# Routed attention with a SoLU layer: the hand-written order of five queues and transfers, written anew up to the middle of the third batch

## The chip, the cores and the metric

The kernel runs on one core of a Trainium2 chip. Five engines of that core take part, each with a queue of its own that it works through strictly in order: TensorE (PE in the profile; its weight loads are listed apart as PEld), VectorE (DVE), ScalarE (ACT), GpSimd (POOL) and SyncE (SP), which does no arithmetic here and issues nearly all DMA transfers. The metric is the device time of one execution in microseconds (us). Three executions of the kernel before took 224.7, 224.66 and 224.9 us, a median of 224.7 us.

## The reference

Attention in which a query sees only the keys of its own cluster, and then a feed-forward layer with a softmax-weighted activation (SoLU) and a layer norm. Batch 4, 8 heads, 768 tokens, head size 64, 16 clusters; the layer is 512 to 1024 to 512 on 3072 tokens.

```python
q_assign = np.argmax(np.einsum('bhsd,hcd->bhsc', q_n, c_n), axis=-1)   # q_n, c_n: unit length
k_assign = np.argmax(np.einsum('bhsd,hcd->bhsc', k_n, c_n), axis=-1)
mask = q_assign[:, :, :, None] == k_assign[:, :, None, :]
scores = np.where(mask, scale * np.matmul(q, k.transpose(0, 1, 3, 2)), -1000000000.0)
attn = softmax(scores)                      # written out in full in the reference
x = np.matmul(attn, v)                      # then all heads of a token side by side
h = x @ w_in
solu = h * softmax(h)
ln = (solu - mean(solu)) / np.sqrt(var(solu) + 1e-06) * g_ln
out = ln @ w_out
```

## The kernel before

**The work.** The kernel goes through 16 pairs of heads, (batch 0, pair 0) to (batch 3, pair 3). For a pair, q and k are loaded and turned (by PE in batch 0, by a VectorE block transpose after that), the tokens are compared with the centroids, and the one-hot cluster of each token is put below the 64 rows of q and k, so that one matmul gives masked scores. The scores of all pairs form 288 banks of PSUM; for each bank, PE computes scores, ScalarE takes the exponential, and PE multiplies the exponentials with v. The v tile has a column of ones behind its 64 columns, which gives the row sums; VectorE divides by them. The feed-forward layer takes 128 tokens at a time, 24 groups: a transposing DMA of x, `h` on PE, its maximum on VectorE, an exponential on ScalarE, the product on VectorE, a second transposing DMA, `y` on PE with statistics taken beside it, a scaling on ScalarE or VectorE, and the store.

**The planner.** Nothing in the program is issued in the order of its text. Every piece of work is put with `add` into a list under a name: the kind, and behind it the batch, pair, bank or group. The class `Weave` then reads a text of kinds for every engine (`ORDER["PE"]` and so on). An entry such as `S3` in it takes the next three operations of that kind from those that belong to the engine, in the order in which they were added. So the texts alone set the order of each queue. The table `AWAY` moves single operations to another engine than the one given in `add`. The durations given in `add` (and the model in `run`) only set the order in which instructions of different engines are written out; on the chip, each queue runs on its own and waits for semaphores.

**The kinds that the prediction speaks of**, with the line that issues the work in the profile:

| kind | engine | work | line |
|---|---|---|---|
| `S`, `E`, `V` | PE, ACT, PE | scores of one bank (2 matmuls; in the first 24 banks one narrower matmul); its exponential; 6 matmuls with v | L613, L621, L638 |
| `N` | DVE | reciprocal and product: divides a group of `V` by the row sums | L650, L663 |
| `h`, `hm`, `ex`, `u` | PE, DVE, ACT, DVE | a quarter of the first product of a group (2 matmuls); maximum; exponential; product | L724, L730, L736, L743 |
| `tx`, `tu` | SP | the transposing DMAs of x and of u | L693, L748 |
| `y`, `sc` | PE, ACT or DVE | a quarter of the second product (2 matmuls); scaling | L788, L803, L805 |
| `al` | POOL | two small operations for the scaling | L770, L773 |
| `cl` | PE | comparison with the centroids (8 matmuls) | L453, L458 |
| `ot`, `pl`, `bl` | DVE; POOL, DVE, ACT or SP | one-hot turned; put in its place; a block cleared | L502, L524, L533 |
| `tp`, `xa` | PE, ACT or DVE | turning q and k of batch 0; taking them out of PSUM | L394, L401 |
| `ca`, `cv` | POOL, DVE, ACT | q or k of one head to bf16; v to bf16 | L439 to L443, L542 |
| `z` | POOL | the column of ones of a v tile | L1246 |
| `ld`, `lv` | SP | loads of q and k, of v | L407, L537 |

Three rings matter. A score bank is free again when its exponential is done, and there are three such banks, so `S` waits for the `E` three banks earlier. The first `V` of a group of units waits for the `N` of the group before. The products `y` share one PSUM bank (tag `m`) with `cl`, so each waits for the scaling or the transpose that empties it. There are six v tiles; `z1` to `z5` set the ones in the second to the sixth, each once in the whole kernel, and the first `V` that reads a tile waits for its `z`:

```python
def clear(z):
    nc.gpsimd.memset(v1[z][:, :, :, D:], 1.0)
```

`z5` belongs to the tile of pair (1,1), whose first `V` is the one named `V28.0`. In POOL's text it stands, as counted out to names, in this neighbourhood:

```text
ca1.1.1.1 ca1.2.0.0 ca1.2.0.1 al1 z5 at2 ca1.2.1.0 al2
```

Of the kernel before, what the change touches and what calls it, by code (L numbers as in the profile page):

```python
# [22 lines left out]
class Weave:  # L23
# [21 lines left out]
    ORDER["PE"] = """
        fl wm fl tp2 cp fl2 cl tp fl tp fl4 cl S3 tp2 S2 tp2 cq S2 tp S tp S2 tp S cl S2 V S
        tp S V S V S gt V S V2 S cl S V S V S V S tp S tp S2 tp S V S tp V2 S2 cl S3 V2 S V
        S V S2 V S V2 S2 V S cl S3 V2 S V S V S su S3 V2 S V S V S su S3 V2 S V2 S2 me S3 V2
        S V S V S cl S2 V S V S V2 S2 h S h S2 h2 S V2 S2 h V2 S h S V2 S2 h S V S V S h S h
        S2 V S h V S y2 V2 S2 y V S V S h3 S3 y V3 h V S2 V2 S cl S3 h2 S2 V3 S y2 S V h2 S  # L50
        V y2 S h S V h S2 h S y3 S2 y V3 h S3 cl V2 S V S y S2 y2 S3 V3 S y S2 V3 S2 cl S V
        S2 V2 S h S2 V2 S V S h S2 V2 cl V2 S3 y2 S V S2 V y S2 y V2 S3 h2 S V h S h S2 V h
        S V S V y2 S h V y2 S2 V S h3 S cl V S2 V2 S h V cl S3 h2 V y V S3 y2 V S h V3 S y S
        h S2 h2 S3 V2 y h S V S2 y V3 y S3 h3 y S3 V3 S h S V S V cl S V S h S cl V2 S3 y V2
        S y S2 y V2 S3 h y V S3 V h V2 S3 cl S2 V2 S y3 S2 y S V3 S V S y S2 V S V3 S2 y2 S3
        y V2 S2 h V2 S3 h3 S V S2 V y S V h2 V2 S y S2 y V y S h2 S3 cl h V S2 V3 S h V2 S3
        h2 S y S2 V h S2 V y2 V4 S3 y h S2 h V h V S V S y2 S3 V3 h2 S2 h2 S2 y2 S V S h2 S
        V3 S2 h S h S2 V S y V2 S V y2 S2 h2 S2 h2 V2 S2 V2 y S2 h V2 h V S2 h S V h S3 V2 h
        y S V y3 V h3 S2 y3 S2 y h2 V2 h y h y3 h V h V y4 h ptx h y4 h2 y3 h2 y ptu2 y6 ptu
        y ptu y5  # L60
    """
# [28 lines left out]
    AWAY.update(dict.fromkeys("""  # L90
        ca0.0.1.0.0 ca0.0.1.0.1 ca0.0.1.1.0 ca0.0.1.1.1 pl0.0.0.0.1 pl0.0.1.0.0 pl0.0.1.1.0
        pl1.0.0.0 pl1.0.0.1 pl1.0.1.0 pl1.0.1.1 pl1.1.0.0 pl1.1.0.1 pl1.1.1.0 pl1.1.1.1
        pl1.2.0.0 pl1.2.0.1 pl1.2.1.0 pl1.2.1.1 pl1.3.0.0 pl1.3.0.1 pl1.3.1.0 pl1.3.1.1
        pl2.0.0.0 pl2.0.0.1 pl2.0.1.0 pl2.0.1.1 pl2.1.0.0 pl2.1.0.1 pl2.1.1.0 pl2.1.1.1
        pl2.2.0.0 pl2.2.0.1 pl2.2.1.0 pl2.2.1.1 pl2.3.0.0 pl2.3.1.0 pl2.3.1.1 pl3.0.0.0
        pl3.0.0.1 pl3.0.1.0 pl3.0.1.1 pl3.1.0.1 pl3.1.1.0 pl3.1.1.1 pl3.2.0.0 pl3.2.0.1
        pl3.2.1.0 pl3.3.0.1 pl3.3.1.0 pl3.3.1.1
    """.split(), "POOL"))
# [1182 lines left out]
```

## Time and profile before

| what | value |
|---|---|
| median of three executions | 224.7 us (224.66 to 224.9) |
| the profiled execution, its own time | 224.64 us |
| its span, first to last instruction | 222.7 us |
| granted TensorE clock | 0.997 |
| PE busy, instructions | 216.4 us (97%), 2420 |
| DVE busy, instructions | 196.8 us (88%), 355 |
| ACT busy, instructions | 192.0 us (86%), 372 |
| POOL busy, instructions | 130.3 us (59%), 251 |
| HBM read and written | 23.11 MB, 6.29 MB |

In rows of the profile, L12 is line 12 of the kernel; `out<-in` names the tiles by the program's own names; `xN` counts instructions. A row of the timeline gives the start, the duration, engine, line and operation, and in square brackets how long the engine stood idle before it and what ended that. Matmuls are pipelined and their ends are modelled, so a full busy column of PE does not say that PE lost nothing; the distance from start to start does. Two instructions on ACT or DVE overlap a little, so the mean of one is longer than the step from one to the next. A row of the chain of waits gives the start, the time and the work on the chain that ended last.

### The profile page before, as it was taken

To read this page: it belongs to the slowest core of one execution; us is meant where nothing else is said; L and a number is where in the kernel's file an instruction comes from. 1 tells how busy PE (TensorE), PEld (TensorE's weight loads), DVE (VectorE), ACT (ScalarE), POOL (GpSimd) and SP (SyncE) were. 2 spreads that over 40 slices of the span, in tenths; PEclk is the share of its full clock that TensorE was granted. 3 is DMA by queue.
4 is the path that set the end of the run, shared out by engine and by line. 5 is a ranking of instruction groups with operands and counts; after the bars stand their busy time and mean duration, and the time that the engine had idled before them with its cause. 6 is when DMAs were issued, how large, how long until landed. Compare 5 with 4: busy or idle time off the path is not lost.

```text
span 222.7 us, 6609 instructions
## 1 busy us (share of the span) xinstructions
PE 216.4 (97%) x2420; PEld 147.9 (66%) x2420; DVE 196.8 (88%) x355; ACT 192.0 (86%) x372; POOL 130.3 (59%) x251
## 2 busy tenths in 40 slices
PE   7999999999999999999999999999999999999993
PEld 4667657666766678776677667777677677755452
DVE  4899997999999989999998989887999889888982
ACT  2699999999997999998889898999999998983362
POOL 3699881970887989547678534953895403032331
PEclk9999999999999999999999999999999999999998
DMA  6999989995898989899998999199930434486713
GB/s 148 353 268 261 278 173 316 243 214 99 126 249 140 232 141 175 189 199 174 178 244 146 174 201 191 66 213 202 236 59 16 92 62 129 92 144 161 183 70 133
DMA packets 125679, 38.80 MB, mean 174 GB/s; under 512 B 115016, under 2 KB 121168, under 8 KB 125648
## 3 DMA queue, kind: packets, MB, share of 16 engines
q1 hardware_dynamic: 123904, 37.87, 80.0%
q10 hardware_dynamic: 1744, 0.52, 1.0%
q8 instruction: 19, 0.31, 0.6%
q14 instruction: 12, 0.10, 0.1%
HBM read 23.11 MB, written 6.29 MB: 132 GB/s over the span
## 4 chain that ended last, share of the span: by engine, by line
PE 93%; ACT 1%; DVE 1%; issue 1%; POOL 1%; DVEq 0%; ACTq 0%
PE sps L613 30%; PE hreg L724 18%; PE yps L788 18%; PE ops L638 15%; PE csc L458 4%; PE hreg L394 2%; PE idle_p L832 2%; ACT e L621 1%; PE csc L453 1%; PE hreg L584 1%; PE hreg L788 1%; PE utp L712 0%; PE hreg L594 0%; POOL qk L441 0%; ACT e_sb L736 0%
## 5 line engine op out<-in xcount | busy, mean ns | idle before, releaser
L621 ACT ACTIVATE e<-sps 128x512 bf16<-128x512 f32 (+1 forms) x288 | 148.7, 604 | 10.5 <-PE sps L613 9.3
L613 PE MATMUL sps<-qk 80*128 80x256 bf16 (+5 forms) x636 | 95.6, 264 | 0.8 <-ACT e L621 0.4
L613 PEld LDWEIGHTS <-qk 80*128 80x128 bf16 (+1 forms) x636 | 60.6, 121 | 26.7 <-issue 8.8
L638 PEld LDWEIGHTS <-e 128*128 128x128 bf16 x1134 | 49.9, 97 | 13.4 <-issue 2.7
L638 PE MATMUL ops<-v,e 128*128 128x65 bf16 x1134 | 55.0, 193 | 0.6 <-POOL v L1246 0.6
L724 PE MATMUL hreg<-w_in_sb,xT 128*128 128x512 bf16 x192 | 52.8, 379 | 0.0
L788 PE MATMUL yps<-w_out_c,uT 128*128 128x512 bf16 x184 | 48.9, 379 | 0.0
L524 POOL COPY qk<-oht 32x384 f32<-32x384 f32 (+1 forms) x48 | 24.2, 504 | 20.2 <-DVE oht L502 17.9
L743 DVE TENSOR_TENSOR u<-e_sb,hreg 128x1024 bf16<-128x1024 bf16 (+1 forms) x25 | 29.1, 1168 | 5.0 <-ACT e_sb L736 4.9
L754 DVE BATCH_NORM_STATS2 bs<-u 128x6 f32<-128x512 bf16 x48 | 31.5, 678 | 0.1
L730 DVE TENSOR_REDUCE nmax<-hreg 128x1 f32<-128x1024 f32 x24 | 29.0, 1210 | 2.6 <-PE hreg L724 2.2
L736 ACT ACTIVATE e_sb<-hreg,nmax 128x1024 bf16<-128x1024 f32 x24 | 27.0, 1123 | 4.6 <-DVE nmax L730 4.4
L443 POOL TENSOR_SCALAR qk<-xt 64x768 bf16<-64x768 f32 (+1 forms) x31 | 25.3, 815 | 2.3 <-ACT xt L401 0.3
L441 POOL CAST qk<-xt 64x768 bf16<-64x768 f32 (+1 forms) x30 | 24.2, 807 | 3.8 <-DVE xt L401 1.7
L788 PEld LDWEIGHTS <-uT 128*128 128x128 bf16 x200 | 18.2, 97 | 11.4 <-issue 0.3
L770 POOL TENSOR_SCALAR esq<-es,mv 128x1 f32<-128x1 f32 x24 | 8.6, 358 | 27.5 <-DVE mv L758 19.2
L724 PEld LDWEIGHTS <-xT 128*128 128x128 bf16 x192 | 16.9, 97 | 9.8 <-DVE u L743 0.6
L415 DVE STREAM_TRANSPOSE xt<-raw 128x768 f32<-128x768 f32 x24 | 22.6, 952 | 0.0
L663 DVE TENSOR_TENSOR x<-ops,den 128x256 bf16<-128x256 f32 (+1 forms) x39 | 19.0, 486 | 1.3
L764 POOL TENSOR_SCALAR es<-esum 128x1 f32<-128x1 f32 x24 | 5.3, 223 | 23.4 <-ACT e_sb L736 22.7
L773 POOL TENSOR_TENSOR alpha<-esq,halves 128x1 f32<-128x1 f32 x24 | 13.5, 562 | 2.0
L542 POOL CAST v<-vf 128x384 bf16<-128x384 f32 x27 | 13.9, 528 | 1.0
(84 smaller groups left out, 174.7 us busy)
## 6 DMA issues: line engine op xcount, KB each, us to landing
vf<-in_v_dram SPq DMA_DIRECT2D x16, 384.0 KB, 4.4
out_dram<-y SPq DMA_DIRECT2D x23, 256.0 KB, 2.5
raw<-in_q_dram SPq DMA_DIRECT2D x50, 96.0 KB, 3.8
raw<-in_k_dram SPq DMA_DIRECT2D x50, 96.0 KB, 2.9
w_g<-in_moe_w_out_dram SPq DMA_DIRECT2D x4, 512.0 KB, 7.5
w_st<-in_moe_w_in_dram SPq DMA_DIRECT2D x4, 512.0 KB, 6.2
raw<-in_q_dram SPq DMA_DIRECT2D x3, 384.0 KB, 5.9
raw<-in_k_dram SPq DMA_DIRECT2D x3, 384.0 KB, 6.5
```

The source lines that it names most:

```text
L441: VEC[e].tensor_copy(dst, src)
L443: VEC[e].tensor_scalar(dst, src, scalar1=inv_C, scalar2=1.0, op0=Alu.mult, op1=Alu.mult)
L524: ins = VEC[e].tensor_copy(dst.bitcast(F32), src.bitcast(F32).unsqueeze(1) .to_broadcast([NB, 2, n // 2]))
L613: nc.tensor.matmul(sps_[n, k][:, c0:c0 + w], side(b, h // 2, 1, h % 2, keys)[r], side(b, h // 2, 0, h % 2, slice(s0 * P, s0 * P + w))[r])
L621: nc.scalar.activation(es[n, k][:, :w], sps_[n, k][:, :w], Act.Exp, scale=exp_scale, bias=-exp_scale)
L638: nc.tensor.matmul(opss[g][:, s, :VW], es[n, k][:, c0:c0 + P], v1[slot(b, h // 2)][:, h % 2, kt, :VW], start=(kt == 0), stop=(kt == n_t - 1))
L724: uses(nc.tensor.matmul(hreg[:, at(f, f2)[1], :], xTs[f][:, dc, :], w_in_sb[:, dc, f2 * FF2:(f2 + 1) * FF2], start=(dc == 0), stop=(dc == ...
L730: uses(nc.vector.tensor_reduce(ff[f, "nmax"][:], pair_of(f), axis=AXY, op=Alu.max, negate=True), *both(f))
L736: uses(nc.scalar.activation(ff[f, "e"][:], pair_of(f), Act.Exp, bias=ff[f, "nmax"][:], accum_out=ff[f, "esum"][:]), *both(f))
L743: uses(nc.vector.tensor_tensor(ff[f, "u"][:, at_], ff[f, "e"][:, at_], pair_of(f)[:, at_], op=Alu.mult), *banks)
L754: nc.vector.bn_stats(ff[f, "bs"][:, f2, :], ff[f, "u"][:, f2, :])
L788: ins = nc.tensor.matmul(dst, ff[f, "uT"][:, at(f, f2)[0] * (n_fc // 2) + c, :], w_out_c[:, fc, cols], start=(fc == chunks[0]), stop=(fc = ...
```

## The change

Only the class's texts change: the five `ORDER` texts from their start to a common tail, and `AWAY`. No instruction's shape, buffer or data is altered. The tail that stays as it was begins at `S64.1` on PE, `E64.0` on ACT, `oh3.1` on DVE, `pl3.1.1.1` on POOL and `lv3.3` on SP, that is at 136.85, 136.6, 139.6, 148.0 and 155.4 us of the profiled execution. Ahead of it every queue holds the same work in another order, but for 19 operations that change their engine:

| to | operations |
|---|---|
| ACT, from DVE | `xa0.0.0.0`, `sc6`, `sc8` |
| ACT, from POOL | `ca0.0.1.0.0` (half size), `ca2.2.0.1`, `ca2.3.0.1` |
| DVE, from POOL | `ca1.0.0.0`, `ca2.1.0.1`, `ca2.2.0.0`, `ca2.3.0.0`, `ca3.0.1.0`, `pl0.3.0.1`, `bl1.3`, `zo` (a clearing) |
| DVE, from ACT | `pl0.0.1.0.1` |
| POOL, from DVE | `ca0.0.0.1.0` (half size), `cv2.0.0`, `bl2.2` |
| POOL, from SP | `pl2.3.0.1` |

On ACT, `ca0.0.0.0.1`, which stood ahead of the first `E`, now stands behind the ninth. On POOL, `z5` moves from the 77th place of the queue to the 61st, from behind `al1` to ahead of `at0`:

```text
cv1.1.0 pl1.1.1.0 pl1.1.1.1 z5 ca1.1.0.1 at0 pl1.1.0.0 ca1.1.1.0
```

The diff, cut to the texts of POOL and ACT, the first lines of the others, and `AWAY`:

```diff
     ORDER["SP"] = """
-        ld4 si ld4 lg lv ld2 lv ld3 lo ld lv ld2 lv ld2 lo2 ld3 lo ld4 li ld li3 tx ld lv
-        ld3 lv tx ld3 tu ld8 lv tu tx ld lv ld4 tu ld3 ou ld2 ou ld tu ld12 tu ld4 lv ld2 ou
...
+        ld4 si ld4 lg lv ld3 lv ld2 lo ld lv ld3 lv ld2 lo ld lo2 ld3 li ld3 li3 tx ld3 lv
+        ld3 tx ld lv tu ld4 lv ld3 tu ld tx ld4 tu ld ou ld6 tu ld ou ld6 tu ld4 lv ld3 lv
...
     ORDER["POOL"] = """
-        zo po ca3 z ca pl ca bl pl2 ca bl ca pl sg cv z ca3 cv ca pl cv pl2 ca gs pl2 ca pl
-        z ca2 cv2 z ca2 pl2 cv pl wi ca2 wi pl wi pl wi pl bl cv pl ca pl at pl cv al ca cv
-        pl at ca bl pl cv ca3 al z at ca al ca at ca pl2 bl cv pl2 ca4 at ca2 al ca pl2 bl
-        pl2 cv2 ca3 al at pl2 bl pl2 ca pl al ca3 at cv at pl ca pl2 ca2 pl al cv2 bl cv2
-        pl2 ca pl al pl at al at pl2 ca3 at al bl cv pl2 bl cv2 ca3 pl5 al cv3 at al ca2 cv
...
+        po ca z ca z ca2 pl bl ca pl2 bl pl ca2 sg ca cv ca cv ca pl3 cv z2 ca2 pl2 ca gs cv
+        pl ca cv ca3 pl2 cv ca wi pl wi3 pl3 ca bl cv3 pl2 z ca at pl ca pl ca al cv at bl
+        ca al at ca4 at ca2 pl2 bl pl2 al ca cv ca al pl3 at pl ca3 cv2 al at pl4 cv ca pl
+        bl al ca2 pl at pl bl at pl cv2 pl al pl cv bl at pl ca pl ca at ca al ca cv al pl3
+        cv pl bl cv ca pl2 bl cv al cv ca3 pl3 at pl2 al cv3 at al ca2 cv ca cv ca2 at ca2
...
     ORDER["PE"] = """
-        fl wm fl tp2 cp fl2 cl tp fl tp fl4 cl S3 tp2 S2 tp2 cq S2 tp S tp S2 tp S cl S2 V S
...
+        fl wm tp2 cp fl2 cl fl2 tp2 fl4 cl S3 tp2 S2 tp2 S cq S tp S tp S tp S2 cl S2 V tp
...
     ORDER["DVE"] = """
-        cn xa cb ca tb mx oh ot pl2 tb mx oh ot xa3 cf xa2 ca cv tb xa mx oh gk N ot pl tb
...
+        cn zo cb tb mx oh ot pl2 tb mx oh ot xa3 cf xa2 pl cv tb ca xa mx gk oh N ot pl tb
...
     ORDER["ACT"] = """
-        wa xa3 pl ca E2 xa E8 pl E6 xa E11 xa E49 ex E10 ex E6 ca E4 ex E8 ex E3 sc E5 ca E2
-        ex E25 ex E9 sc E6 ex E5 sc E2 ex E9 ex E8 ex E9 sc E6 ex E18 ex E21 ex E5 sc E3 ex
...
+        wa xa2 ca xa2 pl E2 xa E7 ca E7 xa E11 xa E49 ex E10 ex E7 ca E3 ex E9 ex E sc E5 ca
+        E5 ex E24 ex E12 sc E3 ex E5 sc E2 ex E5 ca2 E3 ex E6 sc E6 ex E7 sc E3 ex E12 sc E7
+        ex E21 ex E5 sc E3 ex E9 ex E7 sc E2 ex E7 ex E8 ex E7 ex E6 sc E ex E2 sc E3 ex E2
...
     AWAY = {}
     AWAY.update(dict.fromkeys("""
-        ca0.0.0.0.1 ca1.1.0.0 ca1.3.1.1 pl0.0.0.1.0 pl0.0.1.0.1 sc23.0 tu22.1 tu23.1
+        ca0.0.0.0.1 ca1.1.0.0 ca1.3.1.1 ca2.2.0.1 ca2.3.0.1 pl0.0.0.1.0 sc23.0 tu22.1 tu23.1
         xa0.0.0.1 xa0.0.1.0 xa0.1.0.0 xa0.2.1.1 xa0.3.1.1
     """.split(), "ACT"))
     AWAY.update(dict.fromkeys("""
-        bl2.2 bl3.1 bl3.2 bl3.3 ca0.0.0.1.0 ca0.2.0.1 ca1.0.1.1 ca3.1.1.0 cv0.0.0 cv0.2.0
-        cv1.2.0 cv2.0.0 cv3.3.0 pl0.0.0.0.0 pl0.0.0.1.1 pl0.1.0.0 pl0.2.1.1 pl0.3.1.1 sc0
-        sc10 sc13 sc17 sc19 sc2 sc23.1 sc3 sc6 sc8 sc9 tu22.0 xa0.0.0.0
+        bl1.3 bl3.1 bl3.2 bl3.3 ca0.2.0.1 ca1.0.0.0 ca1.0.1.1 ca2.1.0.1 ca2.2.0.0 ca2.3.0.0
+        ca3.0.1.0 ca3.1.1.0 cv0.0.0 cv0.2.0 cv1.2.0 cv3.3.0 pl0.0.0.0.0 pl0.0.0.1.1
+        pl0.0.1.0.1 pl0.1.0.0 pl0.2.1.1 pl0.3.0.1 pl0.3.1.1 sc0 sc10 sc13 sc17 sc19 sc2
+        sc23.1 sc3 sc9 tu22.0 zo
     """.split(), "DVE"))
```

The last table, for POOL, loses `ca0.0.1.0.0` and gains `pl2.3.0.1`.

More of the change, by code (lines that the diff above doesn't have):

```diff
@@ L35 @@
+        ld3 tx ld lv tu ld4 lv ld3 tu ld tx ld4 tu ld ou ld6 tu ld ou ld6 tu ld4 lv ld3 lv
+        ld tx ou tu ld4 ou ld3 tx lv ld3 tu ou ld tu ld6 tx ou ld6 tu lv ld5 ou ld3 lv ld tu
+        lv ou tu ld3 tx ou tu pl ld2 tx lv ld2 ou lv ou lv tu tx ou tu pl2 tu2 tx tu tx ou2
+        tx ou tu tx2 ou tu2 ou2 tu2 ou6
     """
     ORDER["POOL"] = """
-        zo po ca3 z ca pl ca bl pl2 ca bl ca pl sg cv z ca3 cv ca pl cv pl2 ca gs pl2 ca pl
-        z ca2 cv2 z ca2 pl2 cv pl wi ca2 wi pl wi pl wi pl bl cv pl ca pl at pl cv al ca cv
@@ L48 @@
[L48 to L59, printed above, removed]
@@ L85 @@
     AWAY.update(dict.fromkeys("""
[L86 to L88 removed]
+        bl1.3 bl3.1 bl3.2 bl3.3 ca0.2.0.1 ca1.0.0.0 ca1.0.1.1 ca2.1.0.1 ca2.2.0.0 ca2.3.0.0
+        ca3.0.1.0 ca3.1.1.0 cv0.0.0 cv0.2.0 cv1.2.0 cv3.3.0 pl0.0.0.0.0 pl0.0.0.1.1
+        pl0.0.1.0.1 pl0.1.0.0 pl0.2.1.1 pl0.3.0.1 pl0.3.1.1 sc0 sc10 sc13 sc17 sc19 sc2
+        sc23.1 sc3 sc9 tu22.0 zo
     """.split(), "DVE"))
     AWAY.update(dict.fromkeys("""
[L91 to L95, printed above, removed]
+        ca0.0.1.0.1 ca0.0.1.1.0 ca0.0.1.1.1 pl0.0.0.0.1 pl0.0.1.0.0 pl0.0.1.1.0 pl1.0.0.0
+        pl1.0.0.1 pl1.0.1.0 pl1.0.1.1 pl1.1.0.0 pl1.1.0.1 pl1.1.1.0 pl1.1.1.1 pl1.2.0.0
+        pl1.2.0.1 pl1.2.1.0 pl1.2.1.1 pl1.3.0.0 pl1.3.0.1 pl1.3.1.0 pl1.3.1.1 pl2.0.0.0
+        pl2.0.0.1 pl2.0.1.0 pl2.0.1.1 pl2.1.0.0 pl2.1.0.1 pl2.1.1.0 pl2.1.1.1 pl2.2.0.0
+        pl2.2.0.1 pl2.2.1.0 pl2.2.1.1 pl2.3.0.0 pl2.3.0.1 pl2.3.1.0 pl2.3.1.1 pl3.0.0.0
         pl3.0.0.1 pl3.0.1.0 pl3.0.1.1 pl3.1.0.1 pl3.1.1.0 pl3.1.1.1 pl3.2.0.0 pl3.2.0.1
```

43 lines of the change are left out of this document (25 added, 18 removed).

## The prediction

> **What bounds the kernel now.** I read the totals first, then busy time by stretch, then the chain of waits, then the timeline where the chain leaves PE. The page:
>
> ```profile
> span 222.7 us, 6609 instructions
> PE 216.4 (97%) x2420; PEld 147.9 (66%) x2420; DVE 196.8 (88%) x355; ACT 192.0 (86%) x372; POOL 130.3 (59%) x251
> ```
>
> Busy time by stretch (start:end and length, then PE, PEld, DVE, ACT, POOL, granted clock, DMA share); the tail that the change leaves alone begins at 136.85:
>
> ```profile
> 9.24:24.00 14.76, 14.76 (x171) 10.58 (x172) 14.11 (x30) 14.25 (x35) 12.40 (x23) 1.00 1.08 278
> 24.00:52.00 28.00, 27.47 (x357) 18.61 (x354) 25.21 (x47) 26.56 (x53) 18.50 (x29) 1.00 0.99 231
> 52.00:67.32 15.32, 14.69 (x167) 10.46 (x166) 14.87 (x25) 15.10 (x30) 10.48 (x21) 1.00 0.95 176
> 67.32:101.00 33.68, 33.68 (x403) 24.45 (x403) 31.89 (x56) 31.76 (x61) 23.88 (x43) 1.00 0.98 178
> 101.00:136.85 35.85, 35.85 (x405) 24.50 (x404) 33.73 (x57) 32.27 (x63) 22.99 (x43) 1.00 0.99 193
> 136.85:222.70 85.85, 82.16 (x888) 55.01 (x884) 72.08 (x125) 68.61 (x129) 37.23 (x77) 0.99 0.56 123
> ```
>
> Three engines are nearly full in the front, not one. From 9.24 to 136.85, ACT is idle for 0.51+1.44+0.22+1.92+3.58 = 7.67 us of 127.61 and DVE for 0.65+2.79+0.45+1.79+2.12 = 7.80; POOL has 39 us to spare. PE's column is full because ends of matmuls are modelled, so its loss has to come from steps. The chain of waits shows steps where PE runs undisturbed:
>
> ```profile
> 9.89 0.66 PE hreg L394 x6
> 32.10 1.00 PE hreg L584 x8
> 38.95 0.86 PE hreg L594 x2
> 42.13 0.78 PE csc L458 x8
> 46.43 0.44 PE sps L613 x4
> 46.87 0.86 PE hreg L724 x4
> 56.23 0.86 PE yps L788 x4
> 57.09 0.37 PE ops L638 x12
> ```
>
> So an `S` costs 0.22, a `V` 0.185, an `h` or `y` 0.43, a `cl` 0.78, a `tp` 0.33. Counting the text from the first `S` (9.24) to `S64.1` (136.85): 181 S of 0.22 and 24 narrower ones of three quarters of that, 130 V, 48 h, 36 y, 13 cl, 12 tp, two of 1.00, one of 0.86 and 0.3 of small ones: 39.8+4.0+24.1+20.6+15.5+10.1+4.0+2.0+0.9+0.3 = 121.3. The stretch took 127.6. About 6.3 us are all that any order could win there, since the change keeps PE's work. In rows over 0.1 us the largest pieces are the one in the next fence (0.8) and 0.6 at 50.8 to 51.5; the rest is small change at about every tenth step.
>
> **The change part by part.** *1. The ones of the sixth v tile.* The chain of waits leaves PE only here for over 2 us, from 65.2 to 67.3; below it two rows of the timeline (start, duration, idle before it):
>
> ```profile
> 65.21 0.84 POOL qk L441
> 66.14 0.35 POOL esq L770
> 66.57 0.57 POOL alpha L773
> 67.13 0.14 POOL v L1246
> 67.32 0.70 PE ops L638 x18
> ```
>
> ```profile
> 66.41 0.10 PEld L638 LDWEIGHTS <-e 128*128 128x128 bf16 x1
> 67.32 0.58 PEld L638 LDWEIGHTS <-e 128*128 128x128 bf16 x17 [0.81 <-issue]
> 55.68 0.50 POOL L524 COPY qk<-oht 32x384 f32<-32x384 f32 x1 [6.88 <-DVE oht L502]
> ```
>
> PE has loaded weights for `V28.0` at 66.41 and stands 0.81 us until `z5` (L1246) is done; `z5` waited on POOL for nothing of its own, only for its place behind `al1`. In the new text it stands third behind `pl1.1.1.0`, the operation of the third row, which waits for `ot1.1`: 55.68+2x0.6+0.2, about 57. That is 9 us of margin, and nothing near it moves by as much. One queue effect speaks against it: `cv1.1.0`, which before stood at 59.57, now precedes these rows, and its load is moved back by three loads; POOL waited 6.88 us there already, so I cost this at nothing (cover gone: the wait would pass to `z5`, still with 9 us). Late next: `V28.0` also needs `cv1.1.1` (POOL, 62.85 before) and its `E`, both over by 65.6. Gain 0.80, bounds 0.3 (if the next `S` wait for `E`) and 0.81.
>
> *2. ACT's start.*
>
> ```profile
> 9.24 0.65 PE L613 MATMUL sps<-qk 80*128 80x384 bf16 x3 [0.28 <-DVE qk L524]
> 9.16 0.53 ACT L439 ACTIVATE qk<-xt 64x384 bf16<-64x384 f32 x1
> 9.60 0.87 ACT L621 ACTIVATE w_in_sb<-sps 128x384 bf16<-128x384 f32 x2
> 36.95 6.23 ACT L621 ACTIVATE e<-sps 128x512 bf16<-128x512 f32 x12 [0.38 <-PE sps L613]
> 49.26 1.12 ACT L736 ACTIVATE e_sb<-hreg,nmax 128x1024 bf16<-128x1024 f32 x1
> 124.36 1.57 ACT L621 ACTIVATE e<-sps 128x512 bf16<-128x512 f32 x3 [0.88 <-PE sps L613]
> ```
>
> The first `E` stands behind `ca0.0.0.0.1` (9.16) and starts 0.2 after its scores; with that cast moved back it can start 0.1 earlier. In the run of exponentials up to 52 us that follows (ACT 95% busy, in the same order as before), a placing of 0.5 on ACT goes to DVE and the 0.5 of this cast comes in: even. What ACT gains, PE has at its `S`: 0.1 to 0.3; I take 0.15. The 0.6 at 50.8 to 51.5 stays: `S22.1` and `S22.2` wait for two `E` that stand behind the 1.1 of `ex0` (49.26), in both orders alike.
>
> *3. Work that changes engines.* Groups (count, then busy, mean ns):
>
> ```profile
> L439 ACT ACTIVATE qk<-xt 64x768 bf16<-64x768 f32 (+1 forms) x3 | 2.2, 733 | 0.1
> L803 ACT ACTIVATE y<-yps,alpha 128x512 f32<-128x512 f32 x13 | 9.0, 695 | 5.5 <-PE yps L788 4.9 <-POOL es L764 0.5
> L805 DVE TENSOR_SCALAR y<-yps,alpha 128x512 f32<-128x512 f32 x10 | 7.4, 736 | 1.0 <-issue 0.5 <-PE yps L788 0.4
> L443 DVE TENSOR_SCALAR qk<-xt 64x768 bf16<-64x768 f32 x2 | 1.1, 567 | 0.0
> ```
>
> ACT gets two full casts (0.83 each, the three rows' 2.2 less the half one's 0.53), a half one and two scalings of 0.70, 3.6 us, less the placing of 0.5: 3.1. The two full casts and both scalings, 3.06, fall into the stretch from 101, where ACT's idle time is 3.58. DVE gets five casts of 0.57 and some 1.4 of placing and clearing, and gives back two scalings of 0.74 and about 1.7 of `xa`, `cv`, `bl` and a half cast: +1.1. POOL is some 5 us lighter and gains nothing by it, since it has 39 to spare. Where does ACT's new work go? Take its tightest piece, from `S53.1` to `S62.2` in the new order. PE has 27 S, 17 V, 7 h, 6 y and 2 cl: 5.9+3.1+5.6+1.6 = 16.2. ACT has from `E53.1` to `E61.2` 26 exponentials of 0.51 (6.23 less a last tail of 0.1, over 12), two `ex` of 1.1 and two scalings of 0.65 in step: 16.8. So ACT is 0.6 longer than PE there. PE's front runs 5% over its steps (127.6 to 121.3); for 16.2 that would be 0.8, which covers the 0.6 unless both fall together. I charge 0.35, bounds 0 and 1.2. Ahead of it (`S26.0` to `S33.1`) 20 exponentials, a cast, two `ex` and one scaling make 13.9 on ACT against 21 S, 14 V, 14 h or y and one cl, 14.0 on PE: no charge.
>
> *4. Transfers and their queue.* SP's loads, `lv`, `tx`, `tu`, `ou` change places by one to four. The one with little room is `tx6`, which `h6.0.0` waits for. Between the end of `V41.1` and `h6.0.0` the old order has 11 S, 4 V and 4 y (4.9 us), the new one 9 S, 4 V, 4 y (4.4). The path across it is the division `N17` (0.6) and the transfer:
>
> ```profile
> DMA to landing us min/median/max: 2.4/3.3/4.5
> L663 DVE TENSOR_TENSOR x<-ops,den 128x256 bf16<-128x256 f32 (+1 forms) x39 | 19.0, 486 | 1.3
> ```
>
> With the median 3.3 and 0.1 of handing over that is 4.0, hidden by 0.4; at 4.5 it costs 0.8. I take 0. `tu2` and `tu3` no longer stand behind a load and a store; their `y` had 2.4 and 1.6 to spare, no gain.
>
> *5. The tail* has the same order and work. It starts with ACT and DVE as far behind PE as the front leaves them; ACT has 17.2 and DVE 13.8 idle in those 85.85 us. I charge 0; bound 0.8.
>
> [...] A DVE cast beside a POOL cast:
>
> ```profile
> 14.23 0.36 DVE L542 CAST v<-vf 128x384 bf16<-128x384 f32 x1
> 14.29 0.66 POOL L542 CAST v<-vf 128x384 bf16<-128x384 f32 x1
> L542 POOL CAST v<-vf x27: 498/504/827, 14.3 to 174.5; 128x384 bf16<-128x384 f32 x27
> L542 DVE CAST v<-vf x5: 360/368/477, 14.2 to 175.1; 128x384 bf16<-128x384 f32 x5
> ```
>
> Here POOL's took 0.66 instead of its median 0.504 while DVE's ran at its usual length; the longest DVE cast is 0.477, 0.11 over the median. [...]
>
> **The sum**, against the profiled execution's own 224.64 (span 222.7 and 1.94 around it; the median of 224.7 is 0.06 above): -0.80 -0.15 +0.35 = -0.60, so 224.04; as a median 224.1.
>
> **The rivals.**
>
> *A. ACT hands the gain back: no change.* The 0.8 us at 67 also let ACT catch up. For the front to end 0.6 earlier, ACT's idle time from 9.24 to 136.85 must fall from 7.67 to 7.67-3.1-0.6 = 4.0. For: banks are but three, so ACT starves when PE runs long without an `S`; the 0.88 at 124.36 follows 1.7 us without one. Against: the new order's longest such run from 101 on is 1.4, where three banks hold 3x0.51. With 0.6 more idle the time is 224.7.
>
> *B. ACT becomes the bound: slower.* The same place, decided where ACT's idle time in the front stays above 4.6+0.4: in the stretch 24 to 52, where ACT did set the pace, 5% of it was idle, which over 127 us is 6.4. Then the front ends 6.4-4.0 = 2.4 later than forecast, 226.4; half of it gives 225.3.
>
> [...]
>
> *D. More than forecast.* The small change, 6.3-0.8-0.6 = 4.9, shrinks too. With three tenths of it, 1.5: 222.6.
>
> **How the numbers follow.** A measurement of this kernel tells 0.2%, 0.45 us. The forecast case (223.6 to 224.3) gets 0.36, of it 0.3 below 224.25; D (222.6 to 223.6) 0.17; A (224.3 to 225.1) 0.22; B (225.1 to 226.4) 0.18; C 0.07. Faster: 0.3+0.17, 0.47; slower: B, C and a little of A's upper end, 0.28; the rest, 0.25, within. The likeliest case's own range is 223.6 to 224.3; the range that holds eight in ten goes from 222.6 to 225.9.
>
> **What would show it.** `V28.0` no longer waits for L1246, and its `z5` lies at about 57: part 1. The first `E` at 9.5: part 2. ACT's idle time from the first `S` to `S64.1` near 4.0 and that stretch near 127.0: part 3; near 5 or above, with PE's rows on L613 naming `E` around 115 to 125: A or B. `h6.0.0` naming no DMA: part 4. [...] The prediction is wrong if PE waits at a new place for more than 0.5, or if `S64.1` comes after 136.85.

## The result, and the profile after

The changed kernel took 225.32 us (median of 22 executions, 224.04 to 226.91), the kernel before 224.68 (22 executions, 223.88 to 225.59). The ratio is 1.0034, with a 95% interval of 1.0018 to 1.0051: 0.76 us slower, where 0.6 us faster was forecast. Ratios are taken over the fast executions alone and medians over all of them, so a ratio is not the quotient of two medians (the slow ones took 226.57 to 229.09 us at granted clocks of 0.989 to 0.999, and none is among these 44).

Three kinds that the table of kinds does not name come up below: `xt`, DVE's block transpose of a loaded q or k tile (L415); `ou`, the store of an output (L815); `me`, a product on PE that prepares the weights.

The profiled execution of the changed kernel is its slowest, 226.91 us. What it shows has to be divided into what every execution has and what this one had alone. From the page, and busy time by stretch (start:end and length, then PE, PEld, DVE, ACT, POOL, granted clock, DMA share, GB/s):

```profile
span 224.8 us, 6591 instructions
PE 217.7 (97%) x2420; PEld 148.3 (66%) x2420; DVE 197.8 (88%) x358; ACT 194.3 (86%) x377; POOL 124.8 (55%) x244
```

```profile
10.88:26.00 15.12, 15.12 (x183) 11.06 (x180) 14.37 (x32) 14.35 (x35) 12.45 (x23) 1.00 1.03 258
26.00:54.00 28.00, 27.43 (x360) 18.71 (x357) 26.30 (x49) 26.48 (x53) 17.66 (x26) 1.00 0.93 217
67.61:101.00 33.39, 33.39 (x398) 24.20 (x397) 32.49 (x58) 32.10 (x63) 21.34 (x40) 1.00 0.86 167
101.00:109.00 8.00, 6.87 (x68) 3.99 (x65) 6.30 (x9) 6.15 (x13) 4.74 (x10) 1.00 0.93 188
109.00:138.93 29.93, 29.93 (x350) 20.66 (x349) 28.28 (x48) 29.02 (x56) 16.78 (x31) 1.00 1.07 180
138.93:224.80 85.87, 82.22 (x883) 54.90 (x881) 72.15 (x125) 68.36 (x129) 37.27 (x78) 1.00 0.57 132
10.88:138.93 128.05, 126.35 (x1498) 88.47 (x1495) 121.13 (x214) 121.53 (x241) 82.96 (x146) 1.00 0.96 193
```

The first `S` comes at 10.88 (9.24 before) and `S64.1` at 138.93 (136.85). So 1.64 us were lost ahead of the first `S`, and the front takes 128.05 instead of 127.61. One stretch stands out: from 101 to 109 PE, DVE and ACT are all idle for more than a us, which has no counterpart before. The timeline there (start, duration, idle time before it and what ended that):

```profile
97.28 1.75 SPq L407 DMA_DIRECT2D raw<-in_q_dram  x3
102.88 0.98 DVE L415 STREAM_TRANSPOSE xt<-raw 128x768 f32<-128x768 f32 x1 [1.40 <-issue]
103.78 0.93 DVE L441 CAST qk<-xt 64x768 bf16<-64x768 f32 x1
104.83 0.42 DVE L663 TENSOR_TENSOR x<-ops,den 128x256 bf16<-128x256 f32 x1
105.18 1.21 DVE L743 TENSOR_TENSOR u<-e_sb,hreg 128x1024 bf16<-128x1024 bf16 x1
105.31 0.54 PE L638 MATMUL ops<-v,e 128*128 128x65 bf16 x12 [0.77 <-DVE x L663]
106.44 1.04 PE L724 MATMUL hreg<-w_in_sb,xT 128*128 128x512 bf16 x4 [0.36 <-DVE u L743]
```

DVE stands still for 1.40 us ahead of the transpose `xt2.3.0`. The page's word for what ended that is "issue", but the issues of SP tell it: the last piece of the load `ld2.3.0` is the third of the three at 97.28. It was issued at 98.51 and landed at 102.80, and the transpose started 0.08 later. Before, it was the second of the two at 88.48: issued at 88.99, landed at 93.77 and used at 98.33, ahead of both transposing DMAs. The rows of before:

```profile
88.48 2.96 SPq L407 DMA_DIRECT2D raw<-in_q_dram  x2
92.56 1.24 SPq L693 DMA_TRANSPOSE xT<-x  x1
95.70 1.23 SPq L748 DMA_TRANSPOSE uT<-u  x1
98.33 0.96 DVE L415 STREAM_TRANSPOSE xt<-raw 128x768 f32<-128x768 f32 x1
```

Behind the transpose on DVE stand a cast, the division `N19` and a `u`; PE waits for the division at `V46.0` and for the `u` at `h7.1.0`. Counted in steps from start to start against the usual step, these cost PE 0.94 and 0.53 us.

Why was the load late? SP's queue in the execution of the changed kernel:

```profile
93.51 1.24 SPq L693 DMA_TRANSPOSE xT<-x  x1
94.80 0.58 SPq L815 DMA_DIRECT2D out_dram<-y  x1
96.00 1.23 SPq L748 DMA_TRANSPOSE uT<-u  x1
```

In the new text, three of the four pieces of `ld2.3.0` stand three and four places later, behind `tx6`, which SP could not issue until the division `N17` was done at 93.48, and behind `tu5`, which waited for `u5` until 95.94. The load itself needed nothing after 64.12, when the last reader of its buffer, `xt1.3.0`, was done.

A second late place lies in the tail, whose own text is unchanged:

```profile
155.79 0.40 SPq L537 DMA_DIRECT2D vf<-in_v_dram  x1
156.88 0.96 POOL L542 CAST v<-vf 128x384 bf16<-128x384 f32 x2 [3.68 <-DMA vf<-in_v_dram]
159.27 0.98 DVE L415 STREAM_TRANSPOSE xt<-raw 128x768 f32<-128x768 f32 x1
159.75 0.69 ACT L803 ACTIVATE y<-yps,alpha 128x512 f32<-128x512 f32 x1 [0.45 <-DMA vf<-in_v_dram]
```

The loads `lv3.1` and `lv3.2`, issued at 137.46 and 147.41 before, come at 153.10 and 155.79. Among them stand the last pieces of `ld3.3.1` (landed at 159.19 instead of 153.32) and the store `ou9` (landed at 159.68), for whose buffer the scaling `sc11` at 159.75 waits. But the factor that `sc11` needs as well (`al11`, POOL) was done at 159.64 only, so this trace does not tell which of the two held it. `cl3.3`, which needs the bank that `sc11` empties, waits 0.52 us instead of 0.19. The tail as a whole is not longer for it: 85.87 us against 85.85.

### The profile page after: what moved, and what is told of

It is laid out like the page before. It is cut to its first block, busy times and chain, and to the rows that moved or that the text cites. A ratio compares the mean times of both kernels' runs of the same rounds, so it can differ in the third digit from the quotient of the medians.

```text
span 224.8 us, 6591 instructions
## 1 busy us (share of the span) xinstructions
PE 217.7 (97%) x2420; PEld 148.3 (66%) x2420; DVE 197.8 (88%) x358; ACT 194.3 (86%) x377; POOL 124.8 (55%) x244
## 4 chain that ended last, share of the span: by engine, by line
PE 80%; POOL 5%; DMA 4%; SPq 3%; issue 2%; ACT 2%; DVE 2%; DVEq 0%; ACTq 0%; POOLq 0%
PE sps L613 25%; PE hreg L724 16%; PE yps L788 15%; PE ops L638 13%; PE csc L458 5%; PE hreg L394 3%; SPq L407 2%; ACT e L621 2%; DMA vf<-in_v_dram 2%; POOL qk L524 2%; DMA raw<-in_q_dram 1%; DMA raw<-in_k_dram 1%; PE hreg L584 1%; PE idle_p L832 1%; PE hreg L788 1%
## 5 line engine op out<-in xcount | busy, mean ns | idle before, releaser
L613 PE MATMUL sps<-qk 80*128 80x256 bf16 (+5 forms) x636 | 96.3, 264 | 0.5 <-ACT e L621 0.2
L613 PEld LDWEIGHTS <-qk 80*128 80x128 bf16 (+1 forms) x636 | 60.4, 121 | 27.9 <-issue 8.9
L724 PE MATMUL hreg<-w_in_sb,xT 128*128 128x512 bf16 x192 | 53.4, 379 | 0.4 <-DVE u L743 0.4
L788 PE MATMUL yps<-w_out_c,uT 128*128 128x512 bf16 x184 | 50.0, 379 | 0.0
L524 POOL COPY qk<-oht 32x384 f32<-32x384 f32 (+1 forms) x49 | 24.9, 507 | 23.6 <-DVE oht L502 17.8
L415 DVE STREAM_TRANSPOSE xt<-raw 128x768 f32<-128x768 f32 x24 | 22.8, 958 | 1.8 <-issue 1.4
L443 POOL TENSOR_SCALAR qk<-xt 64x768 bf16<-64x768 f32 (+1 forms) x29 | 23.2, 801 | 1.9
L441 POOL CAST qk<-xt 64x768 bf16<-64x768 f32 (+1 forms) x25 | 20.2, 807 | 5.3 <-ACT xt L401 4.2
L542 POOL CAST v<-vf 128x384 bf16<-128x384 f32 x28 | 15.0, 542 | 13.6 <-DMA vf<-in_v_dram 12.9
L803 ACT ACTIVATE y<-yps,alpha 128x512 f32<-128x512 f32 x15 | 10.5, 701 | 5.4 <-PE yps L788 4.9
```

The source lines that it names most:

```text
L415: nc.vector.transpose(xt[:], raws[b, p, i][:].rearrange("p j c -> p (j c)"))
L443: VEC[e].tensor_scalar(dst, src, scalar1=inv_C, scalar2=1.0, op0=Alu.mult, op1=Alu.mult)
L524: ins = VEC[e].tensor_copy(dst.bitcast(F32), src.bitcast(F32).unsqueeze(1) .to_broadcast([NB, 2, n // 2]))
L613: nc.tensor.matmul(sps_[n, k][:, c0:c0 + w], side(b, h // 2, 1, h % 2, keys)[r], side(b, h // 2, 0, h % 2, slice(s0 * P, s0 * P + w))[r])
L724: uses(nc.tensor.matmul(hreg[:, at(f, f2)[1], :], xTs[f][:, dc, :], w_in_sb[:, dc, f2 * FF2:(f2 + 1) * FF2], start=(dc == 0), stop=(dc == ...
L788: ins = nc.tensor.matmul(dst, ff[f, "uT"][:, at(f, f2)[0] * (n_fc // 2) + c, :], w_out_c[:, fc, cols], start=(fc == chunks[0]), stop=(fc = ...
```

## The experiments

The theory after this: the new order puts loads behind transposing DMAs that wait, and that alone ate the gain. The rivals: ACT or DVE is the bound, so that removing these waits brings others; or the opening of PE is slower. All times are medians of 12 executions and the ratio is to the kernel before, run beside it (35 executions; its medians in the three batches are 224.87, 225.09 and 225.13). The changed kernel itself was not run again beside them, so a comparison with its 1.0034 goes across batches.

**The load ahead of the transposes, in the changed kernel.**

```diff
-        ld tx ou tu ld4 ou ld3 tx lv ld3 tu ou ld tu ld6 tx ou ld6 tu lv ld5 ou ld3 lv ld tu
+        ld4 tx ou tu ld ou ld3 tx lv ld3 tu ou ld tu ld6 tx ou ld6 tu lv ld5 ou ld3 lv ld tu
```

> The changed kernel with one edit: the last three pieces of ld2.3.0 stand ahead of tx6 on SP instead of behind tx6 and tu5. Theory: these pieces wait there for a division and a product, the transpose xt2.3.0 on DVE waits 1.4 us for them at 101.5, and the u and the division queued behind it cost PE 0.94 and 0.53 us. Then V46.0 and h7.1.0 do not wait, the stretch from the first S to S64.1 falls from 128.05 to 126.6 to 126.9, and the time is about 1.2 to 1.5 us under that of the changed kernel, near 224.0. If ACT is the bound in that stretch (rival B), the waits go and others take their place: the time falls by less than 0.5 us.

224.62 us, ratio 0.9976 (0.9951 to 1.0001), against 1.0034 for the changed kernel: 0.58% or 1.3 us gained, as expected, though the time itself is 0.6 above the "near 224.0" (between the medians the gain is 0.70). The timeline of DVE in this kernel:

```profile
100.23 0.97 DVE L415 STREAM_TRANSPOSE xt<-raw 128x768 f32<-128x768 f32 x1
101.12 0.51 DVE L441 CAST qk<-xt 64x768 bf16<-64x768 f32 x1
101.99 0.42 DVE L663 TENSOR_TENSOR x<-ops,den 128x256 bf16<-128x256 f32 x1
102.33 1.21 DVE L743 TENSOR_TENSOR u<-e_sb,hreg 128x1024 bf16<-128x1024 bf16 x1
```

No idle time stands ahead of the transpose, and `V46.0` and `h7.1.0` no longer wait. That holds in the profiles of all seven kernels with this edit. The front is 127.27 us, longer than expected; 0.39 of it is a wait at `me` at 39 us that is at most 0.09 in the others.

**The loads of the tail as before, in the changed kernel.**

```diff
-        lv ou tu ld3 tx ou tu pl ld2 tx lv ld2 ou lv ou lv tu tx ou tu pl2 tu2 tx tu tx ou2
+        lv ou tu ld3 lv tx ou tu lv pl ld4 ou2 tx lv tu tx ou tu pl2 tu2 tx tu tx ou2
```

> The changed kernel with one edit on SP: the loads around 140 to 157 us (lv3.1, lv3.2, the four pieces of ld3.3.1, two stores) stand again in the order they had before the change. Theory: the last piece of ld3.3.1 lands at 159.2 instead of 153.3, the DVE transpose xt3.3.1 starts on its landing, and cl3.3 costs PE 0.5 to 1.1 us where it cost 0.2. Then cl3.3 waits at most 0.25 us and the time is 0.3 to 0.9 us under that of the changed kernel, with the two waits at V46.0 and h7.1.0 (1.47 us) still there: 224.5 to 224.9. Rival: something else is late there too (the cast of v on POOL), and cl3.3 still waits over 0.5 us.

225.2 us, ratio 1.0009 (0.9979 to 1.0038). Against 1.0034 that is 0.25%, 0.56 us, inside the 0.3 to 0.9 expected but less than the width of the interval, and the time itself is above the 224.5 to 224.9. In the profiled execution `ld3.3.1` lands at 153.40, so that part is right. But `cl3.3` still waits 0.50: the rival that something else is late there has the better of it. It is `sc11` again, which here waits for its factor (`al11`, POOL) alone. The other five kernels with these loads as before show 0.49 to 0.50 too; with the loads late it was 0.52 in the changed kernel, and 0.66, 0.86 and 1.11 in three others. From `S64.1` to the end the profiles took 85.6 to 85.8 us with the loads as before and 85.87 to 86.3 with them late. So the late loads cost the tail 0 to 0.5 us, and the time does not show it clear of the interval. The waits at `V46.0` and `h7.1.0` were 0.24 and 0.53 in this profile, not the 1.47 in sum that was expected to stay.

**Both edits.**

> Both edits of SP's order, ld2.3.0 ahead of tx6 and the loads of the tail as before. If late loads are all that the new order lost, the gain of z5 and of the small waits is left: about 0.8 to 1.2 us under the kernel before, 223.5 to 224.0. If ACT or DVE is the bound (rival B), no lower than 224.4.

223.98 us, ratio 0.9948 (0.9917 to 0.9978): 1.1 us faster than the kernel before, and the two gains add up within the intervals (0.58% and 0.25% against 0.86%). Beside it in the same batch stands the kernel with the tail's loads alone, so the load ahead of the transposes is worth 0.61% here, 1.4 us by the ratios and 1.2 by the medians. The front, then the tail:

```profile
9.52:136.42 126.90, 126.33 (x1494) 88.65 (x1495) 121.12 (x215) 121.47 (x241) 82.96 (x147) 1.00 0.96 198
136.42:222.20 85.78, 82.14 (x883) 54.98 (x881) 72.19 (x125) 68.39 (x129) 37.63 (x78) 1.00 0.59 134
```

The front takes 126.90 (127.0 was forecast), with ACT idle for 5.43 us in it. That is above the 5.0 at which rival B has the front end later, and yet the front ends earlier: rival B falls. This is also a version that beats both kernels.

**Two casts off ACT**, on top of both edits.

```diff
-        E5 ex E24 ex E12 sc E3 ex E5 sc E2 ex E5 ca2 E3 ex E6 sc
+        E5 ex E24 ex E12 sc E3 ex E5 sc E2 ex E8 ex E6 sc
...
-        ca0.0.0.0.1 ca1.1.0.0 ca1.3.1.1 ca2.2.0.1 ca2.3.0.1 pl0.0.0.1.0 sc23.0 tu22.1 tu23.1
+        ca0.0.0.0.1 ca1.1.0.0 ca1.3.1.1 pl0.0.0.1.0 sc23.0 tu22.1 tu23.1
...
-        bl al ca2 pl at pl bl at pl cv2 pl al pl cv bl at pl ca pl ca at ca al ca cv al pl3
+        bl al ca2 pl at pl bl ca at pl cv2 ca pl al pl cv bl at pl ca pl ca at ca al ca cv al pl3
```

> As the kernel with both edits of SP's order, and ca2.2.0.1 and ca2.3.0.1 on POOL again instead of ACT, so that ACT has 1.66 us less between 108 and 115. The prediction charged 0.35 us for ACT's new work. If that was right, the time is 0.2 to 0.4 us lower than without this edit; if ACT's work there is hidden, it is the same within 0.2 us, with no wait over 0.15 us on PE between S53.1 and S62.2 in either kernel.

223.9 us, ratio 0.9948 (0.9917 to 0.9978), the same as without this edit: the two casts cost nothing on ACT. PE's waits between `S53.1` and `S62.2` sum to 0.56 us here, 0.57 with the casts on ACT and 0.51 in the kernel before, none above 0.1. The stretch with the casts on ACT, then without:

```profile
114.80:131.74 16.94, 16.94 (x206) 12.15 (x203) 16.42 (x27) 16.93 (x35) 10.76 (x21) 1.00 1.02 182
114.60:131.53 16.93, 16.93 (x206) 12.14 (x203) 16.62 (x27) 16.81 (x34) 10.52 (x21) 1.00 1.05 182
```

This edit does not test the 0.35 that the prediction charged, though: the casts run ahead of `S53.1`, and what the prediction counted from there on, exponentials, two `ex` and two scalings, stays on ACT in both kernels. ACT is full there, as the prediction read, and still the stretch takes PE only 4.6% more than its steps of 16.2, as much as the whole front (126.90 to 121.3). So the 0.35 is not seen; no run takes `sc6` off ACT to show it.

**`z5` alone, in the kernel before**, in two places.

```diff
-        pl at ca bl pl cv ca3 al z at ca al ca at ca pl2 bl cv pl2 ca4 at ca2 al ca pl2 bl
+        pl at ca bl pl cv z ca3 al at ca al ca at ca pl2 bl cv pl2 ca4 at ca2 al ca pl2 bl
```

> The kernel before with one edit: the ones of the sixth v tile (z5) stand three casts and al1 earlier on POOL. If the wait of 0.8 us at V28.0 was worth what the prediction took for it, the time is 0.6 to 0.8 us lower, about 223.9 to 224.1, with S64.1 at 136.0 to 136.3. If ACT hands the gain back (rival A), V28.0 no longer waits, but S64.1 stays within 0.2 us of 136.85 and the time within 0.2 us of 224.7.

> The kernel before with z5 where the changed kernel has it, right behind pl1.1.1.1 on POOL, and nothing else. Expected as for the first run of this kind: V28.0 no longer waits for POOL and the time falls by 0.6 to 0.8 us, if no transfer is late in the profiled execution; within 0.2 us of the kernel before if ACT hands the gain back.

The second puts `z` into `pl z cv al ca cv`, a line higher. Ratios 0.9984 (0.9957 to 1.0011) and 0.9971 (0.9937 to 1.0006): 0.4 and 0.65 us, the right way and below the 0.8, neither clear of its interval. The medians, 225.1 and 224.42, lie 0.2 above and 0.7 below that of the kernel before, so in time the gain is not shown. The second's profile has `z5` at 60.61 and `V28.0` without a wait:

```profile
60.61 0.18 POOL L1246 MEMSET v<- 128x96 bf16 x1
69.58 0.60 PE L613 MATMUL sps<-qk 80*128 80x256 bf16 x4
70.02 0.71 PE L638 MATMUL ops<-v,e 128*128 128x65 bf16 x18
```

The wait does not come back next door. But both profiled executions were disturbed elsewhere: the transposing DMA `tx0` took 7.2 and 7.7 us (4.5 in the kernel before), and `h0.0.0` waited 1.1 and 1.7 us for it. So the end points of these two traces cannot be set against 136.85. In the first, `h6.0.0` also waited 1.16, as `tx6` went out at 93.76 and took 4.5 to land. In the second, the granted clock fell to 0.79 from 47.00 to 54.98, behind the wait of 1.7, and the trace is undisturbed from there on. So the way from `S22.2` to `S64.1` can be compared, in the kernel before and in this one:

```profile
51.49:136.85 85.36, 84.72 (x975) 59.64 (x975) 81.00 (x138) 79.64 (x153) 57.35 (x105) 1.00 0.97 183
54.98:139.57 84.59, 84.59 (x975) 59.66 (x974) 81.18 (x138) 79.53 (x153) 56.88 (x105) 1.00 1.01 184
```

It is 0.77 us shorter: nearly all of the 0.80 is still there at `S64.1`, and ACT does not hand it back in the front. The tail behind it takes 85.83 and 85.85 in these two. That speaks against rival A, in one trace.

**The load late, in the kernel before.**

```diff
-        ld3 lv tx ld3 tu ld8 lv tu tx ld lv ld4 tu ld3 ou ld2 ou ld tu ld12 tu ld4 lv ld2 ou
-        tx ld3 tu ou ld2 tx lv ld tu ld4 tx ld tu ou2 ld lv ld4 tu ld4 tu ld ou ld7 pl ou ld
+        ld3 lv tx ld3 tu ld8 lv tu tx ld lv ld4 tu ld3 ou ld2 ou ld tu ld12 tu ld4 lv ou
+        tx tu ld5 ou ld2 tx lv ld tu ld4 tx ld tu ou2 ld lv ld4 tu ld4 tu ld ou ld7 pl ou ld
```

> The kernel before with one edit: the last two pieces of ld2.3.0 stand behind tx6 and tu5 on SP, as in the changed kernel. If the place of this load is what cost the changed kernel its gain, xt2.3.0 waits for it at 98 to 101 us, PE waits 0.8 to 2.0 us more between 98 and 108, and the time rises by that, to 225.5 to 226.7. If the old order has enough room on DVE, the time stays within 0.3 us.

225.61 us, ratio 1.0020 (0.9992 to 1.0048): 0.5 us slower, at the lower end of what was expected and not clear of the interval. DVE waits as expected, with the releaser named this time:

```profile
99.53 0.98 DVE L415 STREAM_TRANSPOSE xt<-raw 128x768 f32<-128x768 f32 x1 [1.05 <-DMA raw<-in_q_dram]
```

and PE waits 0.62 us at `V46.0`, the same place as in the changed kernel. The wait is smaller than expected: `tu5` was issued at 94.86 here and the load landed at 99.45, while in the changed kernel SP was 1.1 us later and the load took 4.3 us to land instead of 2.7.

**PE's opening.** Three kernels. The opening of before in the changed kernel:

```diff
-        fl wm tp2 cp fl2 cl fl2 tp2 fl4 cl S3 tp2 S2 tp2 S cq S tp S tp S tp S2 cl S2 V tp
+        fl wm fl tp2 cp fl2 cl tp fl tp fl4 cl S3 tp2 S2 tp2 S cq S tp S tp S tp S2 cl S2 V tp
```

> The changed kernel with PE's opening up to the first S as it was before: one filling matmul ahead of the first transposes, one between the last two, two fewer elsewhere. Theory: without the filling matmul PE stands idle ahead of the transposes and its steps stay twice as long until 10.6 us. If the order of the opening is the cause, the first S starts at 9.2 to 9.6 instead of 10.88 and the time falls by about 0.6 us or more against the changed kernel. Rival: the first q and k tiles only landed late in that one execution (4.48 us against 3.59); then the time is that of the changed kernel within 0.3 us, and the step lengths change at the same time as in a run with the opening of the changed kernel.

225.77 us, ratio 1.0019 (0.9990 to 1.0049): not to be told from the changed kernel. The rival holds as to place: the first `S` comes at 9.21 with this opening, and with the changed kernel's own opening at 9.13, 9.00, 9.52, 9.38 and 9.58 in five other kernels. The 10.88 was that execution. With the load ahead of the transposes and this opening together (next expectation) it was 224.84, ratio 0.9985 (0.9961 to 1.0009): higher than expected, and on the side that the expectation gives to an ACT that is the bound; its profiled execution, 223.87, lies on the other. The kernel with both edits of SP's order decides that (223.98). Against 225.77 in the same batch, the load ahead of the transposes gains 0.34% here, 0.8 us by the ratios and 0.9 by the medians.

> Both edits in one. If the two losses are separate and nothing else in the new order costs time, they add up: 223.0 to 223.8. If ACT is the bound, no lower than 224.4.

Then both edits of SP's order, with `fl wm tp2 cp cl tp2 cl` (no filling) and with `fl wm fl3 tp2 cp fl3 cl fl2 tp2 fl4 cl` (more):

> The changed kernel with both edits of SP's order, and without eight of the nine filling matmuls of PE's opening (they write a bank that nobody reads). Theory: PE's steps halve only after a stretch in which PE was busy nearly all the time, at 5 to 7 us in most executions; with holes from 4 to 9 us the halving comes later, at 8.5 to 12 us, and the first S starts at 10 to 11 us instead of 9.0 to 9.5: the time is 0.5 to 1.5 us higher than with the two edits alone. Rival: the steps halve at a time that does not depend on PE's work; then the first S starts at 9.0 to 9.5 and the time is the same or 0.1 to 0.2 lower.

> As above, but with four filling matmuls more than the changed kernel, three of them between the first six and the first transposes, where PE stood idle for 0.7 us in the changed kernel's profile. Theory: no hole, the steps halve by 7.3 us in every execution, the first S starts at 9.0 to 9.5; the median is that of the two edits alone within 0.3 us, with no execution above 225. Rival: the transposes start up to 0.4 later behind the fillers and the time rises by that.

The timeline of PE without filling:

```profile
3.96 1.85 PE L394 MATMUL hreg<-ident_f,raw 128*128 128x128 f32 x6
7.31 1.54 PE L394 MATMUL hreg<-ident_f,raw 128*128 128x128 f32 x6
8.78 1.35 PE L458 MATMUL csc<-xt,c_bd 128*32 128x192 f32 x8
10.06 0.66 PE L613 MATMUL sps<-qk 80*128 80x384 bf16 x3
10.56 0.71 PE L394 MATMUL hreg<-ident_f,raw 128*128 128x128 f32 x5
```

A transpose steps at 0.213 us at 8.0 and at 0.109 at 10.6: the halving comes at about 10, and the first `S` at 10.06, though the first tiles landed early here (3.83). That is the place the theory gave. With more filling the halving came at 5.8 and the first `S` at 9.33. In time, 224.27 and 223.82 us, ratios 0.9945 (0.9915 to 0.9975) and 0.9933 (0.9908 to 0.9959): the difference is too small for these intervals, and neither "0.5 to 1.5 us higher" nor "none above 225" came true (two of twelve were, with more filling).

**The transpose ahead of the division**, on top of both edits.

```diff
-        oh hm u bn ag N xt hm bn2 bl tb u ot ag N hm mx bn2 u bn N oh ot hm bl2 u ag N cv hm
+        oh hm u bn ag xt N hm bn2 bl tb u ot ag N hm mx bn2 u bn N oh ot hm bl2 u ag N cv hm
```

> The changed kernel with both edits of SP's order, and on DVE xt3.3.1 ahead of N29 instead of behind it. Theory: with the loads in place, cl3.3 still waits 0.5 us because xt3.3.1 stands behind the division N29 (0.74) on DVE, and the V that needs N29 stands behind cl3.3 and h on PE. Then cl3.3 waits under 0.15 us, nothing new waits, and the time is 0.3 to 0.45 us lower than with the two edits alone: 223.3 to 223.8. If the product, the transfer of u or the V behind it is late instead, the time does not change.

224.3 us, ratio 0.9954 (0.9927 to 0.9981): no gain over both edits. This theory fell. `xt3.3.1` is done 1.0 us ahead of `cl3.3`, and `cl3.3` waits 0.50 all the same:

```profile
157.36 0.57 POOL L773 TENSOR_TENSOR alpha<-esq,halves 128x1 f32<-128x1 f32 x1
157.96 0.69 ACT L803 ACTIVATE y<-yps,alpha 128x512 f32<-128x512 f32 x1 [0.43 <-POOL alpha L773]
158.70 0.85 PE L458 MATMUL csc<-xt,c_bd 128*32 128x384 f32 x8 [0.34 <-ACT y L803]
```

It waits for the bank `m`, which `sc11` empties, which waits for the factor from POOL. SP showed the price of the first edit in this execution:

```profile
88.71 4.75 SPq L407 DMA_DIRECT2D raw<-in_q_dram  x4
93.55 1.23 SPq L693 DMA_TRANSPOSE xT<-x  x1
```

Four pieces took SP 4.75 us (2.77 with both edits alone), so `tx6`, ready at 92.25, went out at 93.55, and `h6.0.0` waited 0.9 us. The two kernels with other fillings, profiled on the same chip, waited 0.85 and 0.70 there. `tx6` is the DMA that the prediction called tight.

## Why the prediction was wrong, point by point

**The step that failed** is part 4, "SP's loads, `lv`, `tx`, `tu`, `ou` change places by one to four. The one with little room is `tx6`". Places were counted, and room was worked out for the transposing DMAs alone. Three pieces of `ld2.3.0` moved by three and four places, past `tx6`, a store and `tu5`, and two of these are DMAs that wait for DVE. (The "one to four" is not so for all: ten operations of SP moved by six places or more.) The rows of before held the numbers: `u5` was done at 94.72, so `tu5` could go at about 95; it takes 1.2 to issue, three issues of 0.6 follow, and a landing takes 2.7 to 4.8; the last piece lands between 100 and 102, against a transpose that started at 98.3 then and starts at 100.2 in the new order with the load in time. This term was taken as 0. In the changed kernel's profile it measured 0.94 and 0.53, together 1.47 us of waits at PE (the same in the kernel with the opening of before, 0.77 in the one with the tail's loads), none in the seven profiles with the load in time, and 0.8 to 1.4 us of time when undone, in three pairs of kernels. What part 4 said of `tx6` held: it landed in 3.1 us, and `h6.0.0` did not wait.

**Part 5**, the tail at 0 (bound 0.8), held in this profile (85.85 and 85.87 us), though by luck. PE's text of the tail is old, but loads, stores and v tiles for it are issued in the rewritten part of SP, and PE's waits in the tail rose from 2.01 to 2.33 us. That does not reach the end: PE's last product came 4.21 us ahead of the end before and 3.88 after. In other profiles the late loads cost up to 0.5, and putting them back gave 0.25%, inside its interval.

**Part 1** was right. `z5` ran at 58.27 (about 57 was forecast, with a first `S` 1.64 earlier) and `V28.0` does not wait; two runs of it alone gave 0.4 and 0.65 us for the 0.80 by their ratios, and the trace of the second keeps 0.77 up to `S64.1`. Its "`cv1.1.0` at nothing" held too.

**Part 2** had the wrong pieces: the first `E` starts 0.37 us behind the first `S`, 0.36 before, so the 0.15 was not there. But the 0.6 that "stays" at `S22.1` and `S22.2` fell to 0.24.

**Part 3**, 0.35 for ACT's load, is not seen: PE takes 4.6% over its steps in the stretch charged, no more than elsewhere, which is the cover that the prediction named. No run took the charged work away. ACT's busy time in the front rose by 1.59 us (119.94 to 121.53), where the prediction added up 3.1; why is not shown.

**Rivals.** B predicted the right side, and with half of its cost even the time (225.3), by a wrong mechanism; that is luck. ACT's idle time in the front was 6.5 us, "near 5 or above", but no row of L613 named `E` between 115 and 125, and without the late loads the front came to 126.90. A would have had no change, 224.7, and the gain of `z5` was still there at `S64.1`. D did not happen: PE's waits in the front other than `S8.0`, `S22.1`, `S22.2`, `V28.0`, `V46.0` and `h7.1.0` sum to 5.50 us before and 5.47 after, so rewriting hundreds of places gained nothing there. C's 0.07 stood for a slower kernel by a late DMA and by DVE casts beside POOL casts, and was half right. A late DMA did cost time, at the neighbour of `tx6`. No run shows a DVE cast held for the whole of a POOL cast (0.82 for L441); what the changed kernel shows is a loss of part of one, beside these two POOL rows:

```profile
102.57 1.73 POOL L443 TENSOR_SCALAR qk<-xt 64x768 bf16<-64x768 f32 x2
104.36 0.71 POOL L524 COPY qk<-oht 32x384 f32<-32x384 f32 x1
```

The DVE cast at 103.78 took 0.93 us, 0.38 more than the median of five such casts (0.557). It started when the upper POOL row had 0.52 left. The lower one started when the cast had 0.35 left, and took 0.21 more than its median of 0.50. So in these two pairs the one that started second lost what was left of the first, less 0.14, and here that stood right between the late transpose and the division. Another DVE cast of this execution, at 34.59, agrees: it started with 0.33 of a POOL cast (34.41, 0.51) left and took 0.74, 0.18 over the median. So do two DVE casts in the kernel with both edits, of 0.86 and 0.74: they started with 0.45 and 0.33 of a POOL cast left and lost 0.31 and 0.19, while the POOL casts, which were first, kept their 0.51. In the rows of before that the prediction shows, DVE had started first (14.23 against 14.29): there POOL was the second, and lost 0.16 of the 0.30 left. The sum of the prediction has no term for this; the largest loss of a DVE cast here is the 0.38, and why the second loses is not shown.

**The sum, afterwards.** At PE in the front: -0.80 (`V28.0`) -0.37 (`S22.1` and `S22.2`) +0.94 +0.53 make +0.30, where the front was 0.44 longer, and the tail added 0.02. Measured were 0.76 by the ratio and 0.64 between the medians, so 0.2 to 0.5 us are not placed by this profile. The tail's late loads, 0 to 0.5 in other profiles, may hold them; no run shows it. The further 1.64 us of the profiled execution were its opening.

## What to carry to other kernels

A queue that issues DMAs in order is worked out like an engine: a DMA goes out when the last wait ahead of it in the queue is over, plus the issues between, plus its landing, and that time is set against its first user. In the changed kernel the wait of `tu5` ended at 95.94, its issue took 1.23, the last of the three pieces behind it was issued at 98.51 and landed 4.3 later, at 102.80, and its first user started 0.08 behind that. Whoever moves a DMA that needs nothing behind one that waits gives it that wait: this load needed nothing after 64.12, and `xt2.3.0` waited 1.40 us for it. A stretch whose text is unchanged can still get new waits while its loads are issued elsewhere: PE's waits in the tail rose from 2.01 to 2.33 us.
